# Fused attention, gated MLP and mixer on one core: the opening rebuilt (whole-float32 first product, masks by TensorE, keys copied by GpSimd, a new order)

## The chip, the cores and the metric

The kernel runs on one core of one Trainium2 chip. The metric is the device time of one execution in microseconds. Everything is one launch: attention, then a gated MLP with a spatial mix, then a token mixer and a channel mixer.

## The reference, cut to what matters

```python
# q, k, v: (4, 8, 576, 64); a causal window of 64 keys
scores = 0.125 * q @ k^T;  scores = where(0 <= t - s < 64, scores, -1e9)
x = softmax(scores) @ v                        # heads joined: (4, 576, 512)
h = relu(x @ w_in);  u, v = h[..., :512], h[..., 512:]       # w_in (512, 1024)
v_n = (v - mean(v)) / sqrt(var(v) + 1e-6)      # over the 512 features
v_s = einsum('ts,bsd->btd', w_spatial, v_n) + b_spatial
x = (u * v_s) @ w_out
h = relu(x^T @ w_tok1) @ w_tok2;  u = x + h^T                # mixes the 576 tokens
out = u + relu(u @ w_ch1) @ w_ch2              # mixes the 512 channels
```

The weights of the two MLPs arrive as 64-bit floats; the kernel takes them apart into 32-bit words itself.

## The kernel before, in words

**Arithmetic.** A product is held accurate by splitting each operand into a rounded part in the reduced float32 format that TensorE takes in one pass (`hi`) and the rest (`lo`), and adding three products, hi·hi, hi·lo and lo·hi (`mm3`, L200). Scores, transposes and probability-times-value use plain float32 operands.

**Attention turns.** The queries are cut into 18 turns of 128 rows. For each pair of batches p there are nine: `i = 0` takes the two 64-row tails of the two batches, `i = 1..8` the eight whole tiles. Before the change they run in the order 0 to 17. A turn n has these steps, whose names appear in the prediction: `Lq` loads queries and keys (L265 for a tile, 640 KB; L267 for tails, 768 KB); `Lv` loads values (L272, 512 KB); `S` is the 32 score matmuls (L295), which run on quarters of the array; `M` on DVE adds the mask and takes the row maximum (L309, per half of the heads, so eight instructions a turn); `X` on ACT is the exponential with its row sum (L318); `I` on DVE is the reciprocal of the sums (L326, L327); `N` multiplies it in, on POOL for turns 0 to 9 (`EARLY`) and on DVE later (L330); `T` transposes (L520) and `C` copies out of PSUM (L525 on DVE or L527 on ACT, by `CD0` and `CD1`); `V` is the 32 matmuls with the values (L338); `xh` and `xl` split the result (L585 ACT, L590 DVE). Then `v`, the 12 matmuls 128x512 with the right half of `w_in` (L200), and for each three turns four `u` products of 12 matmuls 128x384 with its left half. `v` goes on to `R` (relu, ACT), `bn` (DVE), `rs` (POOL), `ts` (DVE, L392), `hi` (ACT) and `lo` (DVE, L398). Spatial products `s` follow when a batch has all its tiles.

**`w_in`.** It comes in eight pieces of 512 KB: `w_v` 0 to 3 (rows of the right half) and `w_u` 0 to 3. A piece is loaded into a spare stretch of the big tile `U` (`wL`, L444), scaled by ACT (`wd`, L153), joined from its two words by two DVE instructions (`wo`, L453 and L454), rounded by ACT (`wh`, L457) and its rest taken by DVE (`wl`, L459). Seven pieces are formed in a PSUM bank of the ring `mm`, which has three; piece `u1` (`PU`) is formed in place in SBUF, with its rest taken by POOL (L472 to L477).

**Who decides the order.** `plan()` states every step of this stage with an engine, a rank, a planned duration, what it comes after and what buffers it takes (`sp` 4 PSUM banks, `xo` 1, `mm` 3, `qk` 2 and `v` 2 buffers, and so on), and `Steps.run()` lists the steps in time by those planned numbers. Each engine then executes its steps in exactly that order, waiting in line for each. The queue SP has a fixed list for the first loads (`ORDER` indexes `loads`), into which a load outside the list can go when the head of the list has no buffer yet. `PADS` and `WARM` put stand-in matmuls (`keep_busy`, L247, 128x512 in bfloat16, results unused) into TensorE's order ahead of named steps. After the plan come the rest of the spatial products, the output product, the token mixer and the channel mixer, none of which the change touches.

Of the kernel before, what the change touches and what calls it, by code (L numbers as in the profile page):

```python
# [36 lines left out]
RANK = dict(M=0.96, X=5.22, I=-0.72, N=6.15, T=0.48, C=1.04, xh=3.48, xl=-0.6, R=0.29, bn=3.08, ts=0.44, hi=4.2, lo=5.8, E=1.49, G=-4.23, av=3.48, dv=1.82, au=4.89, du=3.49, aw=2.75, dw=1.67, c2=4.58)  # L37
SLACK = dict(cd=0.38, cs=0.3, ch=2.95, cl=0.35, oh=0.73, ol=0.69, aw=2.46, ws=2.23, sums=0.17, wd=0, X=0, N=0.3, T=0.32, C=0.14, xh=0.03, xl=0.01, R=0.6, bn=1.03, ts=0.21, hi=0.54, lo=1.64, E=0.9, G=0.2)
# [10 lines left out]
class Steps:  # L49
# [14 lines left out]
    def start(self, step):  # L64
        name, eng, rank, us, fn, after, take, give, hold, kb = step
        at = self.clock.get(eng, 0.0)
        lag = self.LAG + SLACK.get(name[0], 0.0)
        for a in after:
            if a not in self.done:
                return None  # L70
            at = max(at, self.done[a] + lag)
        for r in set(take):
            free, n = sorted(self.room[r]), take.count(r)
            if len(free) < n:
                return None
            at = max(at, free[n - 1] + self.LAG)
        return max(at, self.lands[-8 + (kb > 520)]) if kb else at

    def run(self):
        while True:  # L80
# [32 lines left out]
def tile_kernel(ctx, tc, qk, qkE, v, w_u, w_v, wsT, b_sp, w_out, w_t1, w_t2, w_c1, w_c2, outT):  # L113
# [22 lines left out]
    const.tile([P, 24], F32, name="gap")  # L136
# [112 lines left out]
    its = [(p, i) for p in range(B // 2) for i in range(9)]  # L249
    held, vheld, soft, xt, vn = {}, {}, {}, {}, {}  # L250
# [5 lines left out]
    def qk_parts(t, n):  # L256

        width = 192 if its[n][1] else 256
        return t[:, :512].rearrange("p (j t) -> p j t", j=4), t[:, 512:512 + 4 * width].rearrange("p (j k) -> p j k", k=width)

    def load_qk(n):
        p, i = its[n]
        t = att.tile([P, 1536], F32, tag="qk", name="qk")
        if i:
            nc.sync.dma_start(out=t[:, :1280], in_=qk[8 * p + i - 1])  # L265
        else:
            nc.sync.dma_start(out=t, in_=qkE[p])  # L267
        held[n] = qk_parts(t, n)

    def load_v(n):  # L270
        t = att.tile([P, 1024], F32, tag="vv", name="vv")
        nc.sync.dma_start(out=t, in_=v[n])  # L272
        vheld[n] = (t[:, :512], t[:, 512:])

    def scores(n, pad=0):

        p, i = its[n]
        if n >= len(its):  # L280
            return
        qq, kk = held.pop(n)
        step = 64 if i else 128
        which = 1 if i and where(p, i)[1] == 0 else 0
        on_pe = n < MASK_PE
        scs = [psa.tile([P, 4, 128], F32, tag="sp", name="sc") for _ in range(2)]
        keep_busy(pad, scs[0])
        if on_pe:
            for sc in scs:
                nc.tensor.matmul(sc, ident16, msk16[:, which].unsqueeze(1).to_broadcast([P, 4, 128]), start=True, stop=False)  # L290
        for j in range(4):
            for q in range(2):
                for e in range(2):
                    er = slice(64 * e, 64 * e + 64)
                    nc.tensor.matmul(scs[e][64 * q:64 * q + 64, j, :], qq[er, j, 64 * q:64 * q + 64],  # L295
                                     kk[er, j, step * q:step * q + 128], start=not on_pe, stop=not on_pe or j == 3)
        pb = att.tile([P, 8, 128], F32, tag="pb", name="pb", bufs=PB)
        nm = att.tile([P, 8], F32, tag="nm", name="nm", bufs=3)
        sm = att.tile([P, 8], F32, tag="sm", name="sm", bufs=3)
        soft[n] = (scs, pb, nm, sm, None if on_pe else msk16[:, which])  # L300
# [20 lines left out]
    def snorm(n, g=None):  # L321
        pb, sm = soft[n][1], soft[n][3]
        hs = slice(0, 8) if g is None else slice(4 * g, 4 * g + 4)
        w = hs.stop - hs.start
        rs = att.tile([P, 8], F32, tag="rs", name="rs", bufs=4)[:, :w]
        nc.vector.tensor_scalar(out=rs, in0=sm[:, hs], scalar1=1e-9, scalar2=None, op0=ALU.add)  # L326
# [3 lines left out]
        eng.tensor_tensor(out=pb[:, hs, :], in0=pb[:, hs, :], in1=rs.unsqueeze(2).to_broadcast([P, w, 128]), op=ALU.mult)  # L330
# [43 lines left out]
    def uv_v_mm(p, i, ps):  # L374
# [3 lines left out]
        mm3(ps, [(xh[:, k, ts_], xl[:, k, ts_], wi_h[:, k, 512:], wi_l[:, k, 512:]) for k in range(4)], late=(0, 1, 2) if p + i > 1 else (0, 2, 1))  # L378

    def norm_parts(p, i, ps, vv):  # L380
# [9 lines left out]
        nc.gpsimd.tensor_tensor(out=rstd, in0=rstd, in1=mhalf, op=ALU.pow)  # L390
        yield
        nc.vector.tensor_scalar(out=vv, in0=vv, scalar1=mv[:, 0:1], scalar2=rstd, op0=ALU.subtract, op1=ALU.mult)  # L392
        yield
        if i:
            h, l = turn(nh_ring), turn(nl_ring)
            nc.scalar.copy(out=h, in_=vv)
# [5 lines left out]
        for at in (0, 64):  # L402
            h, t = turn(nh_ring), turn(tail_ring)
            nc.scalar.copy(out=h[at:at + 64], in_=vv[at:at + 64])
            nc.scalar.copy(out=t[:64], in_=vv[at:at + 64])
            hs.append((h, t))
        yield
        for at, (h, t) in zip((0, 64), hs):
# [32 lines left out]
    def w_part(raw, src, hi, lo, cols):  # L441

        raw = raw.bitcast(I32)
        nc.sync.dma_start(out=raw, in_=src.bitcast(I32))  # L444
        r3 = raw.rearrange("p (a c w) -> p a c w", a=4, w=2)
        low, high = r3[:, :, :, 0], r3[:, :, :, 1]
        yield
        ps = psmm.tile([P, 512], F32, tag="mm", name="mm")
        y = ps.rearrange("p (a c) -> p a c", a=4)
        down(y, high)  # L450
        yield
        y = y.bitcast(I32)
        nc.vector.tensor_scalar(out=y, in0=y, scalar1=3, scalar2=None, op0=ALU.logical_shift_left)  # L453
        nc.vector.scalar_tensor_tensor(out=y, in0=low, scalar=29, in1=y, op0=ALU.logical_shift_right, op1=ALU.bitwise_or)  # L454
        yield
        v3 = ps.rearrange("p (k c) -> p k c", c=cols)
        nc.scalar.copy(out=hi, in_=v3)  # L457
        yield
        nc.vector.tensor_tensor(out=lo, in0=v3, in1=f(hi), op=ALU.subtract)  # L459

    def wu_pool(ft):

        fs = slice(128 * ft, 128 * ft + 128)
        raw = U[:, ft, :1024]
# [10 lines left out]
        nc.scalar.copy(out=hi, in_=x)  # L475
        yield
        nc.gpsimd.tensor_tensor(out=lo, in0=x, in1=f(hi), op=ALU.subtract)  # L477

    def wu_part(ft):
        fs = slice(128 * ft, 128 * ft + 128)  # L480
        return w_part(U[:, ft, :1024], w_u[ft], wi_h[:, :, fs], wi_l[:, :, fs], 128)

    def wv_part(k):
# [890 lines left out]
```

## Time and profile before

| | |
|---|---|
| median of three runs | 612.3 us (612.06 to 615.5) |
| the profiled execution | 610.2 us, of which span 608.4 us |
| PE busy | 599.8 us (99%), 4419 matmuls |
| DVE, ACT, POOL busy | 468.9, 350.0, 135.5 us (77%, 58%, 22%) |
| DMA | 108.06 MB, mean 178 GB/s |
| granted TensorE clock | 1.00 throughout |
| chain that ended last | PE 93%, DMA 4%, DVE 1%, ACT 1% |

The span runs from the first to the last instruction. "Busy" of PE includes the stand-in matmuls, and the end of a matmul in the records includes its way through the array, so a row of matmuls back to back is read by its length in the chain of waits rather than by the sum of its members.

### The profile page before, as it was taken

How to read it: one execution, taken by the hardware profiler on the slowest of the kernel's cores; microseconds unless marked ns; L12 is line 12 of the kernel's file. 1: busy time of each engine (PE TensorE's matmuls, PEld its weight loads, DVE VectorE, ACT ScalarE, POOL GpSimd, SP SyncE). 2: the span in 40 equal slices, each digit the busy share in tenths (PEclk: the TensorE clock that was granted, in tenths of full speed). 3: DMA queues.
4: the chain of work that ended last, by engine and by line, in shares of the span. 5: the costliest groups of instructions: out<-in, count | busy, mean ns of one | idle time of the engine just before them, and what ended most of it. 6: DMA issues, size and time to landing. Idle time of an engine off the chain costs nothing.

```text
span 608.4 us, 12236 instructions
## 1 busy us (share of the span) xinstructions
PE 599.8 (99%) x4419; PEld 560.3 (92%) x4419; DVE 468.9 (77%) x1124; ACT 350.0 (58%) x883; POOL 135.5 (22%) x166
## 2 busy tenths in 40 slices
PE   8899999999999999999999999999999999999997
PEld 4688998998898998788988999999999999999997
DVE  5998798989788655594478877878877889786982
ACT  6997678768696334663254445556463647454540
POOL 5342341322233000231046011140012140021310
PEclk9999999999999999999999999999999999999999
DMA  8955269777545803416021314665515675434772
GB/s 351 375 173 181 95 225 312 246 253 267 200 146 210 264 38 94 133 71 207 20 86 63 120 61 145 243 218 209 177 64 192 210 267 169 152 102 176 251 260 79
DMA packets 43093, 108.06 MB, mean 178 GB/s; under 512 B 4372, under 2 KB 14872, under 8 KB 43032
## 3 DMA queue, kind: packets, MB, share of 16 engines
q1 hardware_dynamic: 43032, 107.27, 51.3%
q8 instruction: 35, 0.57, 0.4%
q14 instruction: 26, 0.21, 0.1%
HBM read 86.81 MB, written 20.45 MB: 176 GB/s over the span
## 4 chain that ended last, share of the span: by engine, by line
PE 93%; DMA 4%; DVE 1%; ACT 1%; issue 0%; ACTq 0%
PE mm L200 36%; PE A L1220 19%; PE mm L1008 12%; PE A L1008 9%; PE A L200 6%; PE sc L295 3%; PE sp L520 2%; DMA qk<-in_qk 2%; PE xo L338 2%; PE A L926 1%; PE mm L338 1%; DMA k<-sums 1%; PE A L1304 1%; DMA qk<-in_qkE 1%; DVE pb L309 0%; ACT sh L187 0%
## 5 line engine op out<-in xcount | busy, mean ns | idle before, releaser
L1220 PE MATMUL A<-room,w 128*128 128x384 f32 x720 | 130.0, 334 | 0.0
L1220 PEld LDWEIGHTS A<-room,w 128*128 128x128 f32 x720 | 125.3, 188 | 0.0
L1002 POOL TENSOR_TENSOR hid<-hid 128x384 f32<-128x384 f32 x36 | 42.3, 1186 | 204.0 <-DVE hid L1002 155.6
L1214 ACT CAST room<-hid 128x384 fp32r<-128x384 f32 x120 | 60.9, 513 | 45.4 <-PE A L1220 40.3
L1215 DVE TENSOR_TENSOR room<-hid,room 128x384 fp32r<-128x384 f32 x120 | 71.5, 622 | 12.5 <-ACT room L1214 9.6
L200 PE MATMUL mm<-ws,room 128*128 128x288 f32 x416 | 60.6, 297 | 0.0
L318 ACT ACTIVATE pb<-pb,nm 128x128 f32<-128x128 f32 x144 | 55.8, 393 | 6.9 <-DVE nm L309 6.7
L1033 ACT ACTIVATE hid<-hid 128x384 f32<-128x384 f32 x54 | 28.2, 525 | 53.1 <-DVE hid L1036 53.1
L200 PEld LDWEIGHTS mm<-ws,room 128*128 128x128 f32 x416 | 56.8, 188 | 0.5 <-issue 0.2
L1036 DVE TENSOR_TENSOR hid<-A,hid 128x384 f32<-128x384 f32 x54 | 29.4, 552 | 19.8 <-PE A L1008 14.6
L1008 PE MATMUL mm<-room,sh 128*128 128x384 f32 x144 | 36.5, 334 | 0.0
L309 DVE CUSTOM_DVE_ANT_0 pb<-sc,msk 128x128 f32<-128x128 f32 x144 | 31.5, 284 | 5.8 <-PE sc L295 5.8
L200 PE MATMUL mm<-xh,wi_h 128*128 128x384 f32 x96 | 33.2, 346 | 0.0
L866 POOL TENSOR_TENSOR k<-k 128x256 f32<-128x256 f32 x12 | 9.8, 833 | 105.0 <-ACT gh L907 57.2
L200 PE MATMUL mm<-xh,wi_l 128*128 128x384 f32 x96 | 32.2, 336 | 0.0
L200 PE MATMUL mm<-xl,wi_h 128*128 128x384 f32 x96 | 32.1, 335 | 0.0
L330 POOL TENSOR_TENSOR pb<-pb,rs 128x512 f32<-128x512 f32 x20 | 21.6, 1083 | 41.6 <-DVE rs L327 20.7
L200 PE MATMUL mm<-gh,wo_h 128*128 128x512 f32 (+1 forms) x80 | 30.2, 378 | 0.0
L200 PE MATMUL mm<-gl,wo_h 128*128 128x512 f32 (+1 forms) x80 | 29.6, 370 | 0.2 <-DVE gl L908 0.2
L908 DVE TENSOR_TENSOR gl<-U,gh 128x512 fp32r<-128x512 f32 (+1 forms) x20 | 13.3, 666 | 21.1 <-ACT gh L907 21.0
L200 PE MATMUL mm<-gh,wo_l 128*128 128x512 f32 (+1 forms) x80 | 29.5, 369 | 0.0
L1245 DVE TENSOR_TENSOR U<-A,U 128x384 f32<-128x384 f32 x42 | 21.9, 550 | 9.3 <-PE A L1220 4.7
(183 smaller groups left out, 1507.3 us busy)
## 6 DMA issues: line engine op xcount, KB each, us to landing
w<-scr SPq DMA_DIRECT2D x63, 512.0 KB, 4.1
scr<-raw SPq DMA_DIRECT2D x48, 256.0 KB, 3.2
qk<-in_qk SPq DMA_DIRECT2D x16, 640.0 KB, 6.6
vv<-in_v SPq DMA_DIRECT2D x18, 512.0 KB, 5.4
k<-sums SPq DMA_DIRECT2D x18, 512.0 KB, 3.5
craw<-in_w_c SPq DMA_DIRECT2D x24, 256.0 KB, 3.1
outT<-U SPq DMA_DIRECT2D x24, 192.0 KB, 1.9
k<-in_w_c SPq DMA_DIRECT2D x6, 512.0 KB, 3.5
```

Source lines behind the costliest of these rows:

```text
L200: nc.tensor.matmul(o, a, c, start=(i == 0), stop=(i == n - 1))
L309: nc.vector.tensor_tensor_reduce(out=pb[:, 4 * g + h, :], in0=scs[g][:, h, :], in1=mk, scale=-SCALE, scalar=3e38, op0=ALU.add, op1=ALU.min ...
L318: nc.scalar.activation(out=pb[:, h, :], in_=scs[g][:, h - 4 * g, :] if mk is None else pb[:, h, :], func=AF.Exp, scale=SCALE if mk is None ...
L330: eng.tensor_tensor(out=pb[:, hs, :], in0=pb[:, hs, :], in1=rs.unsqueeze(2).to_broadcast([P, w, 128]), op=ALU.mult)
L1002: eng.tensor_tensor(out=out, in0=a, in1=b, op=ALU.subtract)
L1008: nc.tensor.matmul(o, a, m, start=first and i == 0, stop=i == len(todo) - 1, skip_group_check=True)
L1033: nc.scalar.activation(out=o, in_=src, func=AF.Relu)
L1036: nc.vector.tensor_tensor(out=o, in0=a, in1=b, op=ALU.add)
L1214: nc.scalar.copy(out=oh, in_=blk[j])
L1215: nc.vector.tensor_tensor(out=ol, in0=blk[j], in1=f(oh), op=ALU.subtract)
L1220: nc.tensor.matmul(acc[d], a, m, start=(first and j == 0 and i == 0), stop=(last and j == NJ - 1 and i == 2), skip_group_check=True)
L1245: nc.vector.tensor_tensor(out=at, in0=src, in1=at, op=ALU.add)
```

## The change

- **First product whole.** `NV = 1`: the `v` product of turn 0 is four plain float32 matmuls, 128x512, from a float32 copy of `x` (new ACT step `xf`) and the joined words of `w_v`, in place of twelve of the split kind. It waits for the four `wo` steps, not for `wh` and `wl`; turn 0 still has its `xh` and `xl`, for the `u` products.
- **Masks by TensorE.** `MASK_PE = 3`: for turns 0 to 2 two bfloat16 matmuls 128x512 put the mask into the score banks ahead of the scores; DVE takes the maximum by one `tensor_reduce` per half and scales it, and ACT's exponential reads PSUM and writes SBUF. The banks come free after `X`, not after `M`. Code for this stood in the kernel before, unused.
- **Keys and values.** A tile is laid out as [64 old keys, 128 new keys, queries]. For turns 0 to 5 (`KN = 6`) that are tiles, the old keys are not loaded where they are zeros (POOL `memset`) or lie in the buffer of the turn before (POOL copy, step `Ko`): turns 0, 1, 4 and 5, 128 KB less each. For turns 0 and 1 the 64 rows that both halves of the values share are loaded once and copied by POOL (`Vo`): 384 KB in two DMAs.
- **Order of turns.** `FIRST = (1, 2, 0)`: two whole tiles first, the tails third. Turn 0's queries come in two DMAs of 64 partitions each, and its scores in two steps, one for each (`S 0,0` and `S 0,1`).
- **`w_in` in SBUF.** All eight pieces are formed in place in `U` (`w_piece`), none in PSUM; the rests of `v2` and `u3` are taken by POOL.
- **Later work.** For turns 5 to 13 (`HP`) the `hi` copy of a tile goes from ACT to POOL; for turn 17 (`TA`) ACT normalises in place of DVE; from turn 11 on (`IM`) `I` is one step for both halves; `C` of turns 2 and 3 (first half) and 3 to 5 (second half) is on DVE. The switches `IP`, `TP`, `WP` are empty, so their code does not run.
- **Order.** `ORDER`, `RANK`, `SLACK`, `PADS` and `WARM` are new, and with them the order of every engine in this stage. The loads in SP's list now go: `w_v0`, queries 0 in two halves, values 0, queries 1, `w_v2`, queries 2, `w_v3`, queries 3, `w_v1`, `w_u0`, values 1, `w_u2`, `w_u3`, `w_u1`. Before: queries 0 and 1, `w_v2`, values 0, `w_v1`, `w_v0`, queries 2, `w_v3`, queries 3, `w_u0`, values 1, `w_u2`, `w_u3`, `w_u1`.

The diff, cut to its core:

```diff
-MASK_PE = 0
+MASK_PE = 3
-WARM = 9
-PADS = {("S", 1): 5, ("T", 0, 0): 12, ("T", 0, 1): 3, ("T", 1, 1): 2, ("S", 4): 4}
+WARM = 7
+PADS = {("T", 0, 0): 4, ("S", 2): 7, ("S", 4): 4}
-CD0 = range(0, 1)
-CD1 = range(3, 8)
-PU = (1,)
-ORDER = (0, 2, 5, 4, 3, 1, 7, 6, 10, 9, 8, 12, 13, 11)
+CD0 = range(2, 4)
+CD1 = range(3, 6)
+PV = (2,)
+NV = 1
+FIRST = (1, 2, 0)
+KN = 6
+VN = 3
+HP = range(5, 14)
+IM = 11
+TA = range(17, 22)
+PU = (3,)
+ORDER = (2, 0, 1, 5, 3, 6, 8, 7, 11, 4, 10, 9, 13, 14, 12)
...
+    its = [(0, i) for i in FIRST] + [(p, i) for p in range(B // 2) for i in range(9) if p or i > 2]
...
+    def form_keys(n):
+        old = tile_of(n)[:, :256]
+        if old_keys(n) == "zero":
+            nc.gpsimd.memset(old, 0.0)
+        else:
+            last = qk_tiles[n - 1][:, 256:768].rearrange("p (j k) -> p j k", j=4)[:, :, 64:]
+            nc.gpsimd.tensor_copy(out=old.rearrange("p (j k) -> p j k", j=4), in_=last)
...
+    def form_v(n):
+        va, vb = vheld[n]
+        nc.gpsimd.tensor_copy(out=vb[:64], in_=va[64:])
...
         if on_pe:
-            for sc in scs:
-                nc.tensor.matmul(sc, ident16, msk16[:, which].unsqueeze(1).to_broadcast([P, 4, 128]), start=True, stop=False)
+            for e in es:
+                nc.tensor.matmul(scs[e], ident16, msk16[:, which].unsqueeze(1).to_broadcast([P, 4, 128]), start=True, stop=False)
...
+    def uv_v_whole(x, ps):
+
+        for k in range(4):
+            w = U[:, k, 1152:2176].rearrange("p (c w) -> p c w", w=2)[:, :, 1]
+            nc.tensor.matmul(ps, x[:, 128 * k:128 * k + 128], w, start=k == 0, stop=k == 3)
...
+    def w_piece(raw, src, hi, lo, eng, cast):
+
+        words = raw.rearrange("p (a c w) -> p a c w", a=4, w=2)
+        x, y, low = words[:, :, :, 1], words.bitcast(I32)[:, :, :, 1], words.bitcast(I32)[:, :, :, 0]
+        nc.sync.dma_start(out=raw.bitcast(I32), in_=src.bitcast(I32))
+        yield
+        down(x, y)
+        yield
         nc.vector.tensor_scalar(out=y, in0=y, scalar1=3, scalar2=None, op0=ALU.logical_shift_left)
         nc.vector.scalar_tensor_tensor(out=y, in0=low, scalar=29, in1=y, op0=ALU.logical_shift_right, op1=ALU.bitwise_or)
         yield
-        v3 = ps.rearrange("p (k c) -> p k c", c=cols)
-        nc.scalar.copy(out=hi, in_=v3)
-        yield
-        nc.vector.tensor_tensor(out=lo, in0=v3, in1=f(hi), op=ALU.subtract)
+        (nc.gpsimd.tensor_copy if cast else nc.scalar.copy)(out=hi, in_=x)
+        yield
+        eng.tensor_tensor(out=lo, in0=x, in1=f(hi), op=ALU.subtract)
...
-            nc.scalar.copy(out=h, in_=vv)
+            (nc.gpsimd.tensor_copy if at_turn[p, i] in HP else nc.scalar.copy)(out=h, in_=vv)
...
+            if n < NV:
+                S.add(("v", n), "PE", 10, 3.65, product, after=[("xf", n)] + [("wo", "v", k) for k in range(4)], take=["mm"], give=["vf"], hold=3.5, line="work")
+            else:
+                S.add(("v", n), "PE", 10, 2.95, product, after=[("xl", n)] + [("wl", "v", k) for k in range(4)], take=["mm"], hold=2.83, line="work")
```

## Rows read from the trace of the kernel before

**Rows 1.** Windows: stretch, busy time of each engine (instructions), granted clock, DMA share, GB/s.
```profile
0.00:10.00 10.00, 8.82 (x86) 4.12 (x87) 3.36 (x30) 4.57 (x17) 4.73 (x19) 1.00 0.81 315
10.00:20.00 10.00, 8.41 (x125) 5.39 (x123) 9.66 (x39) 9.98 (x38) 4.12 (x4) 1.00 1.03 387
20.00:30.00 10.00, 8.26 (x120) 6.17 (x118) 9.79 (x49) 10.00 (x41) 4.17 (x4) 1.00 0.97 384
30.00:60.00 30.00, 30.00 (x326) 26.34 (x321) 26.55 (x96) 25.22 (x81) 10.34 (x14) 1.00 0.54 173
```

**Rows 2.** Waits of PE after 29 us: total us, times, longest.
```profile
PE xo L338 <- DVE xl L590: 1.1, 1, 1.1
```

**Rows 3.** Timeline of PE: start, us, engine, line, what, [idle before].
```profile
5.10 1.10 PE L295 MATMUL sc<-qk 64*64 64x128 f32 x32
6.14 1.25 PE L247 MATMUL sc<-warm 128*128 128x512 bf16 x5
...
14.51 1.23 PE L295 MATMUL sc<-qk 64*64 64x128 f32 x32 [0.35 <-DMA qk<-in_qk]
...
16.26 1.15 PE L338 MATMUL xo<-PT,vv 128*64 128x64 f32 x32
...
21.43 1.49 PE L295 MATMUL sc<-qk 64*64 64x128 f32 x32 [0.66 <-DMA qk<-in_qk]
...
24.97 1.17 PE L200 MATMUL mm<-wi_h,xh 128*128 128x512 f32 x4
...
29.03 1.15 PE L338 MATMUL xo<-PT,vv 128*64 128x64 f32 x32 [1.08 <-DVE xl L590]
```

**Rows 4.** Windows, stand-in matmuls (L247) alone.
```profile
0.00:29.03 29.03, 10.40 (x35) 3.40 (x35) 1.00 0.94 361
```

**Rows 5.** Chain of waits, PE: start, us, what.
```profile
49.23 2.76 PE mm L200 x12
51.98 1.08 PE xo L338 x32
...
54.00 1.91 PE sc L295 x64
...
66.66 0.44 PE sp L520 x4
```

**Rows 6.** Chain of waits: the query loads.
```profile
6.29 8.08 DMA qk<-in_qk
...
15.80 5.59 DMA qk<-in_qk
```

**Rows 7.** Timeline of DVE: fourth piece of `w_v`, joined and split.
```profile
20.38 0.69 DVE L454 SCALAR_TENSOR_TENSOR mm<-U,mm 128x512 int32<-128x512 int32 x1
...
23.80 0.68 DVE L459 TENSOR_TENSOR wi_l<-mm,wi_h 128x512 fp32r<-128x512 f32 x1
```

**Rows 8.** By line: what `w_in` costs; count, then ns min/median/max.
```profile
L453 DVE TENSOR_SCALAR mm<-mm x7: 673/689/693, 10.6 to 34.2; 128x512 int32<-128x512 int32 x7
...
L472 DVE TENSOR_SCALAR U<-U x1: 422/422/422, 35.5 to 35.5; 128x512 int32<-128x512 int32 x1
...
L457 ACT CAST wi_h<-mm x7: 581/587/624, 12.0 to 35.9; 128x512 fp32r<-128x512 f32 x7
...
L475 ACT CAST wi_h<-U x1: 677/677/677, 37.5 to 37.5; 128x512 fp32r<-128x512 f32 x1
...
L477 POOL TENSOR_TENSOR wi_l<-U,wi_h x1: 1304/1304/1304, 38.2 to 38.2; 128x512 fp32r<-128x512 f32 x1
```

**Rows 9.** By line: DVE operations between SBUF tiles.
```profile
L392 DVE TENSOR_SCALAR vf<-vf,mv,rstd x18: 516/544/1417, 36.9 to 198.1; 128x512 f32<-128x512 f32 x18
...
L398 DVE TENSOR_TENSOR room<-vf,room x16: 659/684/1221, 48.9 to 201.5; 128x512 fp32r<-128x512 f32 x16
```

**Rows 10.** Timeline of POOL: last constant, first normalisations.
```profile
4.61 1.17 POOL L226 CAST tails<-U 64x512 fp32r<-64x512 f32 x2
...
12.41 2.04 POOL L330 TENSOR_TENSOR pb<-pb,rs 128x512 f32<-128x512 f32 x2 [0.53 <-DVE rs L326]
```

More of the change, by code (lines that the diff above doesn't have):

```diff
@@ L252, in where, with tile_of @@
     def where(p, i):
         return (2 * p + (i - 1) // 4, (i - 1) % 4) if i else (None, None)
[L256 to L261, printed above, removed]
-        p, i = its[n]
-        t = att.tile([P, 1536], F32, tag="qk", name="qk")
+    def tile_of(n):
+        if n not in qk_tiles:
+            qk_tiles[n] = att.tile([P, 1536], F32, tag="qk", name="qk")
+        return qk_tiles[n]
@@ new lines, in old_keys @@
+    def old_keys(n):
+        p, i = its[n]
+        if not i or n >= KN:
+            return None
+        return "zero" if where(p, i)[1] == 0 else "copy" if n and its[n - 1] == (p, i - 1) else None
+    def form_keys(n):
[5 more added lines that the diff above has]
+            nc.gpsimd.tensor_copy(out=old.rearrange("p (j k) -> p j k", j=4), in_=last)
@@ L297, in scores @@
[L297 to L300, printed above, removed]
+                    nc.tensor.matmul(scs[e][64 * q:64 * q + 64, j, :].rearrange("p (w k) -> p w k", w=2), qq[er, 128 * j + 64 * q:128 * j + 64 * q + 64],
+                                     keys_of(n, er, j, q), start=not on_pe, stop=not on_pe or j == 3)
@@ new lines, in load_values, with has_keys, scored @@
+        def load_values(n):
+            part = its[n][1] and n < VN
+            S.add(("Lv", n), "SP", 8 + 2 * n, 0, lambda: load_v(n), take=["v"], hold=0.95 if part else 0.5, kb=385 if part else 512, line="SP" if n < 2 else None)
+            if part:
+                S.add(("Vo", n), "POOL", -1, 0.8, lambda: form_v(n), after=[("Lv", n)], hold=0.75)
+        def has_keys(n):
+            return [("Lq", n)] + [("Ko", n)] * (old_keys(n) is not None)
+        def scored(n, es=(0, 1)):
+            scores(n, S.pad, es)
@@ L558, in block @@
             ahead = [m for m in (n + len(ns), n + len(ns) + 1)[:len(ns)] if m <= last] if len(ns) > 1 else [n + 2]
-            need = [("C", m, g) for m in ns for g in range(2)] + [("Lv", m) for m in ns]
+            need = [("C", m, g) for m in ns for g in range(2)] + [("Vo" if its[m][1] and m < VN else "Lv", m) for m in ns]
             if len(ns) > 1:
-                need += [("Lq", m) for m in ahead]
+                need += [x for m in ahead for x in has_keys(m)]
             else:
@@ L569, in product @@
                 att_pv(m, held.pop(("PT", m)), xo.rearrange("p (j t) -> p j t", j=4))
[L571 removed]
+            take = ["xo"] + ["mm"] * (len(ns) - 1) + ["XT"] * sum(m % 3 == 0 for m in ns) + ["sp", "sp", "pb"] * len(ahead)
             for m in ns:
```

231 lines of the change are left out of this document (140 added, 91 removed).

## The prediction

> **What bounds the kernel now.** I read the busy time by stretch first, then the waits of TensorE (PE), then its timeline over the opening, then the loads.
>
> From 30 to 60 us PE has 30.00 of 30 us busy, while ACT has 25.22 and DVE 26.55 [rows 1]. Past 29 us the longest wait of PE is 1.1 us, and that is the one which ends at 29.03 [rows 2, 3]. From there to the tail the time is PE's work laid end to end, so a step that becomes faster on another engine there buys nothing, and the later part of the change (`HP`, `TA`, `IM`, the copies of `C`) I cost at nothing; its cover is ACT's and DVE's slack of 3 to 5 us in each 30.
>
> Before 29.03 it is otherwise. PE seems busy, but 10.40 us of that are stand-ins [rows 4]. Its real work there is the scores `S` of turns 0 to 4, six half-turn `T`, `V` of two turns and one `v`. At the lengths these have back to back (`S` 1.91/2 = 0.955, `T` 0.44, `V` 1.08, `v` 2.76 [rows 5]) this is 4.78 + 2.64 + 2.16 + 2.76 = 12.3 us. So **16.7 us of the opening are lost**, and the change can win only there. What fills the opening: from 10 to 30 ACT is busy 9.98 and 10.00 of 10, DVE 9.66 and 9.79, the DMA engines all the time at 387 and 384 GB/s [rows 1]. Three resources are full together. The first `v` starts at 24.97 [rows 3], right behind the last rest of `w_v`, which begins at 23.80 and takes 0.68; the words of that piece were joined by 20.38 + 0.69 = 21.07 [rows 7]. The scores of turns 2 and 4 wait for query loads that take 8.08 and 5.59 us from issue [rows 3, 6].
>
> **The change, part by part.**
>
> *Loads.* At 315, 387 and 384 GB/s, 3.15 MB have moved by 10 us, 7.02 by 20 [rows 1]. In the order of issue the queries of turn 2 end at 4.19 MB, which these rates reach at 12.7; they landed at 6.29 + 8.08 = 14.4. Those of turn 4 end at 7.08 MB, reached at 20.2, landed at 21.4 [rows 6]. So a landing is this sum and about 1.5 us. In the new order, with whole tiles first (512 KB, then 384 KB of values, then 512), turn 2 ends at 3.80 MB, turn 3 at 4.98, the fourth `w_v` piece at 5.51, turn 4 at 6.55, values 1 at 6.95. This counts the values of turn 2 ahead of the queries of turn 2, as a load outside the list can slip in while the head has no buffer; without it all are 0.52 MB, 1.4 us, sooner. Landings with it: 13.1, 16.2, 17.5, 20.2 and 21.3. The fourth piece of `w_v`, put behind three turns of queries, lands between 16.1 and 17.5; I take 16.8.
>
> *First product whole.* It needs no `wh` and `wl`, which were 24.97 - 21.07 = 3.9 us of the path. New path: 16.8, then `wd` about 0.6 (the ACT pass over the same 128x512 in SBUF, L475, takes 0.68 [rows 8]), then 0.42 for the shift in SBUF [rows 8] and 0.69 to join [rows 7], and 0.5 for an ACT and DVE that are never idle: **it starts at 19.0**. Its other operand, `xf`, costs ACT one more pass of about 0.59 (L457 [rows 8]) and is ready long before: turn 0's `V` was at 16.26 [rows 3] and comes no later. No row shows a plain float32 matmul of 128x512. Below, the `V` rows: 32 plain float32 matmuls of 64 columns, two at a time on half the array each, in 1.08 us is 1.05 ns a column, and 4 x 512 columns are 2.16 us. Above, four half-products at the rate at which `mm3` does three: 2.76 x 4/3 = 3.68. I take 3.68, as it comes from the row with the same tile: 0.92 more than now; the other end would be 0.60 less.
>
> *Masks by TensorE.* Six bfloat16 matmuls of 128x512 at 0.25 each (five in 1.25 [rows 3]) are 1.5 us on PE. They stand ahead of scores that wait for their queries, where stand-ins stood before; cost nothing. If the cover goes, 1.5. On DVE one reduction over 128x512 (no row; between 0.52, a pass of SBUF [rows 9], and 0.69, one of PSUM [rows 8]) and a small scaling replace four instructions; nothing either way. ACT reads PSUM in place of SBUF; rows for 128x512 casts are 0.587 from PSUM against 0.677 from SBUF [rows 8], so at most a seventh of six half-turn exponentials, 1 us; at least nothing. I take nothing.
>
> *`w_in` in SBUF.* The shift falls from 0.689 to 0.422 [rows 8], 0.27 on DVE for each of about five pieces before 29 us, 1.3. One `wl` moves to POOL, 0.68 off DVE, at 1.30 on POOL [rows 8]. `w_v0` is now the first load and can be taken apart before the first scores, while ACT and DVE have nothing (by 10 us they had worked 4.57 and 3.36 [rows 1]): 2.1 us off DVE's full stretch, 1.2 off ACT's. In sum DVE gets back 4.1 us. ACT gets back 1.2 and pays 0.59 for `xf` and 0.09 more for each cast out of SBUF, some 0.5: nothing in sum. That is why I do not let the stretch end sooner than the loads allow. The freed PSUM banks remove no wait that the rows show.
>
> *Keys and values by POOL, tails third.* The first scores need the keys' `memset`, which stands in POOL's order behind constants that end at 4.61 + 1.17 = 5.78 [rows 10]; the `memset` is at most 0.5. The scores begin at 6.3 in place of 5.10 [rows 3], and end near 8, as one half of the heads fills half of the array at a time. Behind them wait `M`, `X`, and the load of turn 2. SP issues three more DMAs, in time in which it waits for buffers anyway. The late start of `X` costs nothing as long as `V` of turn 0 is not what `v` waits for; ACT uses the time for `w_v0`. `Vo` and `Ko` add some 0.5 to 0.8 us each to POOL, which had worked 4.1 of 10 us [rows 1].
>
> *The sum.* Before 19.0 PE does four `S` (turn 3's queries are there at 16.2), four `T`, one `V`: 3.82 + 1.76 + 1.08 = 6.66. From 19.0 to 29.03 it has `v`, then `T` and `V` of turns 1 and 2, `S` of turn 4, two more `v`, enough to be full but for one wait, for values 1 (21.3) and their split; I put 1 us for it. Useful, measured in the old work: 10.03 - 0.92 - 1 = 8.1. Together 14.8 against 12.3: **2.4 us gained**. Past 29 us nothing changes. The profiled execution took 610.2 us (span 608.4), 2.1 under the median of the three runs; 607.8 for such an execution, **609.9 as a median**.
>
> **Rivals.**
>
> *Everything on time.* The fourth piece lands at 16.1, nothing waits, no gap after: `v` at 17.8, useful 6.66 + 11.2 - 0.92 = 17.0, a gain of 4.6 us, 607.7; with the cheap float32 rate 6.1, 606.2. For it: the path has slack on DVE now. Against it: ACT, full and not relieved.
>
> *The saving in loads is paid back.* Turn 0's queries come as two transfers of 64 partitions, and the values of turns 0 and 1 likewise in parts. No row shows the rate of a large transfer to half the partitions. If each half runs at half the rate, 0.52 + 0.39 MB ahead of everything else cost 1.3 + 1.0 = 2.3 us more, and every later landing slips by it: the gain of 2.4 is gone, 612.2. The Trainium skill's page SBUF — State Buffer ("Can I just issue two DMAs to hit both halves?") says just this: a transfer to partitions 0 to 63 reaches half of the ports, and two such transfers serialize. Against it: the queue holds other whole-width loads at the same time, and its engines were at full rate with loads of several kinds in flight [rows 1].
>
> *Slower: DVE waits for POOL.* A DVE pass between SBUF tiles takes 0.544 as a rule and 1.417 at worst, a subtraction 0.684 and 1.221 [rows 9]; POOL held a 1.04 us instruction in such cases. Seven pieces leave PSUM for SBUF: some 19 DVE instructions that were out of POOL's reach (0.673 to 0.693 without exception [rows 8]) come into it, and POOL's share of the time rises from 4.1 of 10 us to about 6. At 0.6 of the time and some 0.7 us for each meeting (between 0.54 and 0.87), 19 x 0.6 x 0.7 = 8 us are lost, 4.1 got back: the joined words are 3.9 us late, `v` starts at 25.0 as before and pays 0.92, and the second `v`, which still needs all four `wl`, adds a gap of 1: 1.9 slower, 614.2. It decides from about 6.5 us lost, where the gain is gone. The Trainium skill's GPSIMD Engine Reference (Key points) states the contention for two-port modes and for two SBUF inputs, both of which hold here; the rows above agree for the worst cases, but the medians beside them say that most instructions meet nothing, and many POOL instructions lie where DVE reads PSUM.
>
> **How the numbers follow.** A measurement of this kernel can tell about 1% (6 us) from no change. Chances: forecast (gain 0.8 to 3.5) 0.48; everything on time (3.5 to 7) 0.25; loads paid back (within 0.8) 0.13; slower 0.14. The range runs from the far end of the second, with the cheap float32 rate and 1 us for the unknown exponential, 605.2, to the third and most of the last, 614.2. Faster by over 1% (below 606.2) needs that far end, half of the second case: 0.13. Slower by over 1% needs losses past every row here: 0.04.
>
> **What would show it.** In the changed kernel: first plain float32 `v` at 18 to 20 us and 3.7 long, from four matmuls; PE without waits of over 1 us afterwards; stand-ins down to 22, hence less than 7 us; the shifts of `w_in` at 0.42, not 1.0 or more; first scores at 6.3. Wrong if `v` starts past 22, if the second `v` is more than 3 us behind the first's end, or if PE shows waits after 30 us that it had not.

## The result, and the profile after

The changed kernel takes 617.1 us (median of 10 executions, 614.4 to 619.1), the kernel before 612.35 beside it (10 executions): ratio 1.0078 [1.0054, 1.0101]. It is 4.8 us slower; the forecast was 609.9, its range 605.2 to 614.2. The profiled execution of the changed kernel took 619.0 us (span 617.2), 1.9 above its median, as the one of before was 2.1 below its own. The two traces are thus 8.8 us apart, 4 us more than the medians; sizes below that matter are taken from medians, and the traces show places. In the experiments a few executions of 846 us and more, one of them the profiled one of e3, are left out of the medians and ratios.

The busy time by stretch, as in [rows 1] (length of the stretch; PE, PEld, DVE, ACT, POOL; then granted clock, DMA share, GB/s):

```profile
0.00:10.00 10.00, 8.05 (x41) 4.29 (x41) 3.46 (x6) 3.86 (x10) 6.68 (x23) 1.00 0.82 247
10.00:20.00 10.00, 10.00 (x101) 6.02 (x100) 7.03 (x19) 7.72 (x32) 4.50 (x5) 1.00 1.00 360
20.00:30.00 10.00, 7.23 (x122) 5.02 (x122) 7.92 (x31) 9.23 (x34) 3.28 (x5) 0.83 0.84 297
30.00:60.00 30.00, 28.26 (x308) 23.10 (x307) 27.45 (x81) 24.07 (x78) 11.35 (x14) 1.00 0.51 161
```

The three resources that were full together from 10 to 30 us are not so any more: ACT has 7.72 and 9.23, DVE 7.03 and 7.92, and the DMA engines are full from 10 to 20 us and at 0.84 behind. Up to 30 us ACT did 20.81 us of work and DVE 18.41, against 24.55 and 22.81 before. Some of DVE's difference is work that the change saves (shorter shifts, one rest moved to POOL); what is not saved has to be done later. PE, in time, answering to [rows 3]:

```profile
1.04 3.17 PE L261 MATMUL mm<-warm 128*128 128x512 bf16 x7 [1.04 <-DVE warm L138]
4.98 0.58 PE L342 MATMUL sc<-msk,ident 128*128 128x512 bf16 x1 [0.77 <-POOL msk L145]
5.71 1.97 PE L347 MATMUL sc<-qk 64*64 64x128 f32 x16
7.61 0.61 PE L342 MATMUL sc<-msk,ident 128*128 128x512 bf16 x1
8.15 1.97 PE L347 MATMUL sc<-qk 64*64 64x128 f32 x16
10.05 1.03 PE L342 MATMUL sc<-msk,ident 128*128 128x512 bf16 x2
11.02 1.99 PE L347 MATMUL sc<-qk 64*64 64x128 f32 x32
...
17.46 1.10 PE L347 MATMUL sc<-qk 64*64 64x128 f32 x32
...
25.36 1.69 PE L261 MATMUL sc<-warm 128*128 128x512 bf16 x4 [2.77 <-DVE nm L357]
26.98 1.99 PE L347 MATMUL sc<-qk 64*64 64x128 f32 x32
28.89 0.69 PE L572 MATMUL sp<-ident,pb 128*128 128x128 f32 x4
29.52 1.15 PE L394 MATMUL xo<-PT,vv 128*64 128x64 f32 x32
30.60 3.87 PE L440 MATMUL mm<-U,xf 128*128 128x512 f32 x8
```

The first scores are two steps of 1.97, where 32 took 1.10; turn 1's begin at 11.02 in place of 7.32, turn 2's at 17.46 in place of 14.51. At 25.36 a stop of 2.77 ends: stand-ins and scores of turn 4 wait for the banks that the maxima of turn 3 (L357, DVE) give free, and behind them in PE's line stand a `T` of turn 2, `V` of turn 1 and the first `v`, at 30.60 (24.97 before, 19.0 forecast). What DVE and ACT waited for longest from 3 to 30 us (total us, times, longest):

```profile
DVE mx L354 <- PE sc L347: 4.1, 4, 1.7
DVE U L531 <- ACT U L167: 3.9, 1, 3.9
DVE pb L357 <- PE sc L347: 1.3, 1, 1.3
```

```profile
ACT wi_h L534 <- DVE U L532: 2.3, 2, 1.5
ACT U L167 <- DMA U<-in_w_v: 2.2, 1, 2.2
ACT pb L366 <- DVE rs L378: 1.8, 2, 0.9
ACT pb L366 <- DVE nm L361: 1.7, 1, 1.7
```

In the kernel before the two waited in that stretch for the first scores (ACT 4.7, DVE 5.8), and then hardly at all. The gap is whole by 60 us: the first pair of scores (turns 6 and 7) begins at 59.59 in place of 53.93 with one `v` less behind it, 5.66 + 2.76 = 8.4 us of the 8.8. From this pair to the end are 557.6 us here and 556.6 to 559.2 in the traces of e1, e2, e5 to e8, e14, e18 and e19, which put the same work ahead of it: what they gain is gained before it.

### The profile page after: what moved, and what is told of

Read it like the earlier page. It is cut to its first block, busy times and chain, and to the rows that moved or that the text cites. A ratio compares the mean times of both kernels' runs of the same rounds, so it can differ in the third digit from the quotient of the medians.

```text
span 617.2 us, 12189 instructions
## 1 busy us (share of the span) xinstructions
PE 606.2 (98%) x4408; PEld 563.8 (91%) x4408; DVE 469.6 (76%) x1071; ACT 348.3 (56%) x878; POOL 144.7 (23%) x184
## 4 chain that ended last, share of the span: by engine, by line
PE 91%; DVE 4%; DMA 2%; ACT 1%; issue 1%; POOL 0%; SPq 0%; ACTq 0%; POOLq 0%; DVEq 0%
PE mm L214 34%; PE A L1315 19%; PE mm L1103 12%; PE A L1103 9%; PE A L214 6%; PE sc L347 3%; PE sp L572 2%; PE A L1021 1%; DMA k<-sums 1%; PE mm L394 1%; PE xo L394 1%; PE A L1399 1%; DVE U L532 1%; DMA qk<-in_qk 1%; DVE pb L357 1%
## 5 line engine op out<-in xcount | busy, mean ns | idle before, releaser
L366 ACT ACTIVATE pb<-pb,nm 128x128 f32<-128x128 f32 x120 | 46.7, 395 | 4.0 <-DVE nm L357 4.0
L202 DVE TENSOR_TENSOR sl<-k,sh 128x1024 fp32r<-128x1024 f32 x18 | 25.8, 1436 | 2.7 <-PE mm L1103 1.2
```

Source lines behind the costliest of these rows:

```text
L202: eng.tensor_tensor(out=lo, in0=x, in1=f(hi), op=ALU.subtract)
L366: nc.scalar.activation(out=pb[:, h, :], in_=scs[g][:, h - 4 * g, :] if mk is None else pb[:, h, :], func=AF.Exp, scale=SCALE if mk is None ...
```

## The experiments

All times are medians, given in the order of the list above them; each ratio is to the kernel before on the same chip, with its 95% interval.

**Single edits of the changed kernel.** Theory C: the two warm-up products that it dropped let the opening run at the lower rate. Theory P: the stand-ins ahead of turn 4's scores delay the work behind them.

```
e1_warm9           WARM = 7 -> 9
e2_nopad4          PADS without ("S", 4): 4
e3_warm9_nopad4    both
e4_before_warm7    the kernel before: WARM = 9 -> 7
```

> The changed kernel with 9 opening stand-ins in place of 7, nothing else; the planned order is the same. Theory C (cold TensorE): the changed kernel leaves a 0.77 us gap between its last stand-in and the first mask, and runs at the 1.2 GHz length (a 128x512 stand-in 0.47 us, 32 scores 1.99 us) from 5 to about 15 us; with 9 the scores of turn 0 come at full rate, 16 of them in about 1.0 us in place of 1.97, they end near 7.8 in place of 10.1, the load of turn 2 goes out 2.4 us sooner, and the time falls by 2 to 4 us to 613 to 615. Theory D (DVE waits for POOL in SBUF) and theory L (order of loads): the clock is a by-product; below 1 us, 616 to 617.

> The changed kernel without the four stand-ins ahead of the scores of turn 4. They write the score bank, so they wait for the same bank as the scores (PE idle 2.77 us until 25.36) and then run 1.69 us in front of them. Theory P (the stand-ins lie on the path): the scores of turn 4 start at 25.4 in place of 27.0, the first product near 28.9 in place of 30.6, time 1.5 to 2 us less, 615 to 615.6. Rival: the first product waits for the fourth joined piece of w_v (27.8) and the engines behind it, so that below 1 us is gained, 616 to 617; or the clock stays down longer without them, and it is slower.

> Both edits: 9 opening stand-ins, none ahead of the scores of turn 4. If theories C and P both hold and are separate, the two gains add: 3.5 to 6 us, 611 to 613.5. If C removes the wait that P removes, the sum is less than that by over 1 us. If D or L is the cause, 615.5 to 617.

> The kernel before with 7 opening stand-ins in place of 9, nothing else. Theory C: 7 end at about 4.1, the first scores wait for their load until 5.1, TensorE stays at the 1.2 GHz length until the stand-ins ahead of the scores of turn 1 and the first transposes bring it up; the scores of turn 0 take about 2 us, the first product starts 1 to 2 us late, 613 to 614.5. Rival: the gap does not matter there, 612 to 612.6.

Measured: 616.16 (1.0068 [1.0051, 1.0085]); 616.97 (1.0088 [1.007, 1.0106]); 615.2 (1.0054 [1.0036, 1.0071]); 613.22 (1.0019 [1.0005, 1.0033]). With nine warm-up products PE shows:

```profile
5.66 1.09 PE L347 MATMUL sc<-qk 64*64 64x128 f32 x16
6.69 0.39 PE L342 MATMUL sc<-msk,ident 128*128 128x512 bf16 x1
7.01 1.09 PE L347 MATMUL sc<-qk 64*64 64x128 f32 x16
...
26.17 3.87 PE L440 MATMUL mm<-U,xf 128*128 128x512 f32 x8
```

The three scores take 3.28 us in place of 5.93, and `v` comes 4.4 us sooner. This trace is of the fastest of six executions (615.0) and that of the changed kernel of its second slowest (619.0), so the 4.4 stand beside 4.0 us of these two and not beside the medians. By the medians the time gains 1.0 (0.6 by the ratios, with intervals that overlap); the kernel before loses 1.2 [0.3, 2.0] by the opposite edit, so there C is surely something, about 1 us. P is worth nothing that can be told: e2 lies 0.1 under the changed kernel, e3 1.0 under e1, within the intervals.

**Four parts undone, added up.** Theory H: transfers to half of the partitions slow the loads. Rival: POOL's rests hold up DVE.

```
e5_whole_loads    e1; turn 0's queries and the values of turns 0, 1 in whole transfers, no copy by POOL
e6_dve_low        e1; rests of w_v 2, w_u 3 on DVE
e7_whole_scores   e5; scores of turn 0 as one step of 32
e8_four           e1 + e5 + e6 + e7, and no stand-ins ahead of S4
```

> The changed kernel with 9 opening stand-ins, and the queries of turn 0 and the values of turns 0 and 1 loaded over all 128 partitions in one transfer each (128 KB more for each value, no value copy on POOL); the planned order is the same. Theory H (transfers to 64 partitions are slow): from 5 to 10 us the DMA engines are full in both, at 307 GB/s with halves and 407 in the kernel before; here the rate goes back to about 400, the fourth w_v piece lands 1.5 to 2 us sooner, the first product starts near 24.5 in place of 26.2, the time falls by 1 to 2 us from 616.2, to 614 to 615.2. Rival: the rate comes from the rows or from waits for buffers and stays near 310, time 616 to 617.

> The changed kernel with 9 opening stand-ins, and the rests of w_v2 and w_u3 taken by DVE (0.69 us each) in place of POOL (1.3 to 1.75); the planned order of all else is the same. Theory D (DVE waits for POOL in SBUF): POOL's 1.75 us instruction at 18.8 made three DVE instructions wait (0.43, 0.77 and 0.67 us in place of 0.42, 0.69 and 0.16), so the gain is 0.5 to 1 us, 615.2 to 615.7; if contention were the main loss, 2 us or more. Rival: DVE's own 0.69 more in a full stretch cancels it, 616 to 616.6.

> As the run with whole-width loads, and the scores of turn 0 in one step of 32 in place of two of 16. Half the heads use half the rows of the array: 16 take 1.09 us where 32 take 1.10. Expected: the scores of turn 0 end 1 us sooner, the query load of turn 2 goes out 1 us sooner, 0.3 to 1 us off that run. Rival: the fourth w_v piece and the order behind it decide, no change beyond 0.3 us.

> All together: 9 opening stand-ins, whole-width loads, scores of turn 0 in one step, rests by DVE, no stand-ins ahead of the scores of turn 4. If clock, half-width transfers and contention are what the change lost by, the first product starts below 23 us and the time is at the kernel before or under it, 609 to 612.5. If the new order itself (the waits in line behind the scores of turn 4 and the fourth w_v piece) is the cause, it stays above, 613.5 to 615.

Measured: 615.9 (1.0061 [1.004, 1.0081]); 616.0 (1.0067 [1.0044, 1.0089]); 615.89 (1.0059 [1.0037, 1.0081]); 613.92 (1.0036 [1.0021, 1.005]). The stretch from 5 to 10 us, of the changed kernel and then of e5:

```profile
5.00:10.00 5.00, 4.86 (x34) 3.25 (x33) 3.15 (x5) 1.93 (x8) 2.77 (x4) 1.00 1.03 304
```

```profile
5.00:10.00 5.00, 5.00 (x70) 3.34 (x69) 3.71 (x9) 2.48 (x12) 2.14 (x3) 1.00 1.04 415
```

The last column confirms H as a rate, 304 GB/s against 415 (407 in the kernel before) with the DMA engines busy all the time in both. The time does not follow: 0.3 us, within the intervals. None of the three alone moves it; together, with the stand-ins ahead of S4 gone as well, they give back 2.2 (616.2 to 613.9, with intervals that do not overlap). In e8 PE still stops ahead of S4, the scores of turn 4:

```profile
22.59 1.99 PE L352 MATMUL sc<-qk 64*64 64x128 f32 x32 [3.10 <-DVE nm L362]
24.50 1.12 PE L577 MATMUL sp<-ident,pb 128*128 128x128 f32 x4
25.55 1.98 PE L399 MATMUL xo<-PT,vv 128*64 128x64 f32 x32
27.46 4.33 PE L445 MATMUL mm<-U,xf 128*128 128x512 f32 x8
```

A stop of 3.10 is followed by scores of 1.99 (1.10 at the full rate), a `T` of 1.12 (0.66), a `V` of 1.98 (1.15) and a `v` of 4.33 (3.87): 2.6 us more. The granted clock from 22.59 to 27.46 is 0.50, the lower of its two levels (1.2 GHz of 2.4).

**New plans.** Theory L: what is left is PE's line, S4 ahead of `V` and `v`, and DVE's, the maxima of turn 3 ahead of the fourth `w_v` join.

```
e9_join_first          e8:        M(3): after=[... , ("wo", "v", 1)]
e13_after_join_first   changed:   the same line
e10_split              e8:        NV = 1 -> 0
e11_old_order          e8:        RANK, SLACK, CD0, CD1 and ORDER as in the kernel before
```

> The kernel of four undone parts (nine warm-up products, whole loads, unsplit scores, both rests back on DVE, no stand-ins ahead of turn 4's scores), and one line more: the maxima of turn 3 may not be planned ahead of the join of the last w_v piece. On DVE that join then stands ahead of M(3), and on TensorE the scores of turn 4 fall behind V of turn 1 and the first v. Theory L (line): TensorE stood 3.10 us because S4 was in its line ahead of work that was ready, and DVE joined the fourth piece at 24.83 because M(3) was in its line ahead of it; so the first v begins at 22.8 to 24.5 in place of 27.46, TensorE has no wait over 1.5 us from 19 to 30, and the time is 610 to 612 (613.92 without the line). Rival N (new parts cost as such): the wait goes to another instruction and the time stays at 613.5 to 614.5. Rival F (the clock): v begins sooner but runs at 4.3 us or longer, and the time gains under 1 us.

> The changed kernel with that one line alone: the maxima of turn 3 not ahead of the join of the last w_v piece. Theory L: the first v, at 30.60 in the changed kernel, begins at 26 to 28, and the time falls from 617.1 to 613 to 615. Rival N: the fourth piece is late for other reasons (cold opening, half-width loads), v begins past 29 and the time stays at 616 to 617.5.

> The kernel of four undone parts with the whole float32 product undone as well: the first v is made of three products like the others. Theory L: TensorE's line holds the first v behind S4 whichever way it is formed, so the whole product gained nothing of its start; with rests to wait for, v begins at 27 to 29 and the time is 613 to 615. Rival W: the whole product, 0.92 us dearer, is itself the loss: 612 to 613. Rival E (the product does what it is for): v begins 3 us or more later than 27.46 and the time is 615.5 to 617.

> The kernel of four undone parts with the ranks, the allowances, the places of the copies of C and the order of loads of the kernel before. All of the new mechanisms stay: whole product, masks by TensorE, tails third, w_in in SBUF. Theory L: in this line the first v stands ahead of V of turn 1 and the fourth w_v piece is loaded ahead of the queries of turns 2 and 3; v begins at 21 to 24.5 and the time is 610.5 to 613. Rival N: 614 to 616, since the new parts cost as much under any order.

Measured: 618.26 (three executions, 616.9 to 621.1; 1.0111 [1.0074, 1.0147]); 617.16 (1.0087 [1.0065, 1.011]); 617.2 (1.0084 [1.0058, 1.0111]); 620.9 (1.0149 [1.0114, 1.0183]). `v` began at 25.17, 27.11, 34.06 and 23.65. It was earlier in three of them, in e11 and e13 by as much as theory L said and in e9 by 0.7 less, and by its median none is faster: e11 has the earliest `v` of these and the longest time. The theory falls as it was put. These runs settle less than they should, as one line makes a new plan: in e9 PE stops again for 2.25 at 39 us, and it is idle for 2.08 of the 50 us from 150.

**One part alone, the order kept.** Parts of the change put into the kernel before, whose planned order stays as it was; and e8 with eighteen steps moved by hand in the finished plan.

```
e15_before_sbuf    w_part forms the piece in U and not in a PSUM bank
e16_before_masks   MASK_PE = 3 in scores, smax, sexp; 0 in the plan
e17_before_whole   e15; v of turn 0 by four float32 products from U and xf
e14_hand_order     e8; xf, xh, xl of turn 0, C of turn 1, wo of the fourth piece earlier;
                   S4 behind the first v, maxima of turn 4 behind xl of turn 1
```

> The kernel before with one part of the change: all pieces of w_in formed in SBUF and not in PSUM; the planned order is kept to the last instruction. Theory D (DVE meets POOL in SBUF): some shifts, joins and rests are drawn out by 0.3 to 0.9 us, DVE loses 1.5 to 3 us in the opening, the first v begins at 25.5 to 27 (24.97 before), and the time is 613 to 615.5. Rival M (the rows of before: the medians of SBUF passes are shorter): v begins at 24 to 25.2 and the time is 611 to 612.8.

> The kernel before with one part of the change: the masks of three turns by TensorE; the planned order is kept to the last instruction. My prediction costed this at nothing: 611.8 to 612.9. Rival B (banks): with exponentials read from PSUM the banks of the scores come free after X and not after M, some 1.6 us later, so a transposition or the scores of turn 4 begin later: 613.5 to 615.5. Rival G (a gain on DVE, one reduction and a scaling in place of eight passes): 610 to 611.5.

> The kernel before with w_in formed in SBUF and the first product with w_v in whole float32 (one more copy on ACT); the planned order is kept, so the first v stays behind V of turn 1 in TensorE's line. If the whole product does what I predicted, v begins at 22 to 24 and 3.7 long, and the time is 0.5 to 2 us under that of the same kernel without it. If TensorE's line or a join is its gate, v begins past 24.5 and the time is 0.5 to 1.5 us above that kernel's.

> The kernel of four undone parts, with its planned order kept to the last instruction but for eighteen steps around 17 to 27 us that are moved by hand: both copies and the rest of turn 0's output and the C of turn 1 come earlier on ACT and DVE, the words of the fourth w_v piece ahead of those of w_u and of the maxima of turn 3, and on TensorE V of turn 1 and the first v ahead of the scores of turn 4. Theory L (the lines alone): V of turn 1 begins at 20.3 to 21.5 (25.55 without the moves), the first v at 22 to 24 (27.46), no stop over 1.3 us and no stretch at the lower clock between 17 and 30; 609.5 to 611.5 against 613.9 without the moves. Theory D (DVE is too slow, whatever stands first in its line): v at 24 or later, TensorE stops again for 2 us or more before 40 us, 613 to 615.

Measured: 612.82 (1.0 [0.9987, 1.0012]); 615.95 (1.006 [1.0039, 1.008]); 613.39 (1.0012 [0.9996, 1.0028]); 616.12 (1.0055 [1.0036, 1.0074]). The pieces in SBUF cost nothing that can be told (0.0 [-0.8, +0.7]), and neither does the whole product; but it gains nothing here either: `v` begins at 26.77 in the trace of e17 and at 26.66 in that of e15, in both right behind `V` of turn 1 and a `T` in PE's line. The masks cost 3.7 [2.4, 4.9]. ACT in e16, its first two lines:

```profile
8.31 1.28 ACT L319 ACT_TABLE_LOAD   x1 [8.31 <-DVE nm L314]
9.60 0.37 ACT L319 ACTIVATE pb<-sc,nm 128x128 f32<-128x128 f32 x1
```

and PE, two of the waits that are new and the first `v`, 2.98 later than before:

```profile
11.16 2.75 PE L248 MATMUL sp<-warm 128*128 128x512 bf16 x12 [1.24 <-ACT pb L319]
...
23.89 1.02 PE L248 MATMUL sc<-warm 128*128 128x512 bf16 x4 [0.79 <-ACT pb L319]
...
27.95 1.18 PE L201 MATMUL mm<-wi_h,xh 128*128 128x512 f32 x4
```

The first exponential begins 2.89 us later than before (6.71). Of that 1.28 is the table load, which in e16 stands behind the maximum and elsewhere runs at 0.72: a by-product of this edit alone, as in the changed kernel ACT has a piece of `w_v` ahead. Some 1.1 is the two products ahead of the scores, with the scores themselves at 1.43 in place of 1.10, and 0.5 that one reduction ends later than the first of four passes. The two waits for ACT are the rival "banks" of the expectation: exponentials that read PSUM hold the banks until `X`. If the table load costs its whole length, which no run shows, about 2.4 of the 3.7 belongs to the masks. e14 is slower than any of its forecasts; PE:

```profile
23.87 1.73 PE L415 MATMUL xo<-PT,vv 128*64 128x64 f32 x32 [3.36 <-DMA vv<-in_v]
```

With S4 out of the way `V` of turn 1 stops as long, for its values: their load stood behind that of turn 2's values, which had slipped into the list, and so behind `V` of turn 0. Part of the 616.1 goes with the clock: with the same program, the four executions of e14 at a mean granted clock of 1.000 took 614.3 to 615.9, the four at 0.993 or 0.994 616.5 to 618.6.

**The last two.** The masks undone in the changed kernel with its order kept; and e14 with masks undone and the values of turn 1 loaded ahead of turn 2's, those of turn 0 behind two other loads.

```
e18_after_no_masks   MASK_PE = 0 in scores, smax, sexp; 3 in the plan
e19_loads_order      e14 with that, and Lv(1) ahead of Lv(2), Lv(0) behind the second w_v piece
```

> The changed kernel with one part undone: the masks of the first three turns are added by DVE again; the planned order is kept to the last instruction. Theory B (banks): the masks by TensorE cost the kernel before 3.7 us, as exponentials that read PSUM hold the banks of the scores until X, and as their products stand ahead of the first scores. If that is also the changed kernel's loss, the stop ahead of turn 4's scores (2.77 us) and the waits for the masks go, and the time is 612.5 to 615 (617.1 with the masks). Rival O (the order and the loads set the opening whatever frees the banks): 616 to 617.5.

> The kernel with eighteen steps moved by hand, and two changes more: masks on DVE again as in the run beside it, and three loads moved (the values of turn 1 ahead of those of turn 2, which had slipped in front of four other loads and left the values of turn 1 to wait for V of turn 0; the values of turn 0 behind the queries of turn 1 and a w_v piece). Theory B and the loads together: V of turn 1 no longer waits 3.36 us for its values and begins at 20 to 21.5 (23.87 without), the first v at 21.5 to 23.5 and 3.7 long, no stretch at the lower clock from 17 to 30; 608.5 to 611.5, at or below the kernel before. If the wait only moves to a join on DVE, v begins past 24.5 and the time is 612 to 614.5.

Measured: 616.01 (1.0066 [1.0044, 1.0088]), 1.1 under the changed kernel (0.7 by the ratios) with intervals that overlap, and 613.79 (1.0024 [1.001, 1.0038]). PE in e19:

```profile
20.40 1.15 PE L416 MATMUL xo<-PT,vv 128*64 128x64 f32 x32 [1.26 <-DMA vv<-in_v]
21.48 0.66 PE L594 MATMUL sp<-ident,pb 128*128 128x128 f32 x4
21.97 3.76 PE L462 MATMUL mm<-U,xf 128*128 128x512 f32 x8
...
29.99 0.56 PE L369 MATMUL sc<-qk 64*64 64x128 f32 x2 [2.20 <-DVE nm L379]
30.88 1.98 PE L369 MATMUL sc<-qk 64*64 64x128 f32 x30 [0.33 <-DVE nm L379]
32.79 1.98 PE L416 MATMUL xo<-PT,vv 128*64 128x64 f32 x32
34.69 2.08 PE L231 MATMUL mm<-wi_h,xh 128*128 128x512 f32 x4
```

Everything up to 25.66 is where the expectation had it, `v` 3.0 us ahead of the kernel before, ACT with 24.59 us of work by 30 us (24.55 before). Then the scores of turn 5 stop for 2.20 + 0.33 us behind the maxima of turn 4, which I had moved back to make room, and three groups run at the lower rate (granted clock 0.51 from 29.99 to 34.69): 0.88 + 0.83 + 0.90 = 2.6 us more. No version beat the kernel before. Whether this one would with those maxima put forward again was not tried.

## Why the prediction was wrong

The step that failed first is the path to the first `v`, with its term "0.5 for an ACT and DVE that are never idle", and the sum built on it: the gain was reckoned from the start of the first `v`, and its start from the landing of the fourth piece of `w_v` at 16.8 and three passes. In the trace those passes queue. DVE's lines, where the second pair is the fourth piece, and ACT's pass over that piece:

```profile
20.34 1.00 DVE L361 TENSOR_SCALAR nm<-mx 128x4 f32<-128x4 f32 x1
21.26 0.42 DVE L531 TENSOR_SCALAR U<-U 128x512 int32<-128x512 int32 x1
21.71 0.69 DVE L532 SCALAR_TENSOR_TENSOR U<-U 128x512 int32<-128x512 int32 x1
...
26.67 0.41 DVE L531 TENSOR_SCALAR U<-U 128x512 int32<-128x512 int32 x1
27.12 0.69 DVE L532 SCALAR_TENSOR_TENSOR U<-U 128x512 int32<-128x512 int32 x1
```

```profile
24.98 0.68 ACT L167 ACTIVATE U<-U 128x512 f32<-128x512 f32 x1
```

ACT scales it at 24.98, behind a piece of `w_u`, `xf`, `xh` and a `C`; DVE joins it by 27.8 (forecast 19.0), behind `M` of turn 3 and `xl`; and `v` follows at 30.6, behind S4, `T` and `V` in PE's line. The landing was put too early as well: the changed kernel has moved 2.47 MB by 10 us and 6.07 by 20, where the prediction took 3.15 and 7.02 from the kernel before. Its own sum (5.51 MB, and 1.5 us) then gives 19.9, an estimate, as the trace has no landing for this piece. So of the 11.6 us some 3 are the loads and the rest the lines of ACT, DVE and PE. And the start of `v` does not set the time anyway: in the profiled executions of the changed kernel, e1, e8, e19 and e11, `v` at 30.60, 26.17, 27.46, 21.97 and 23.65 went with 619.0, 615.0, 614.0, 614.1 and 619.7, and 24.97 with 610.2 before.

*"The late start of X costs nothing as long as V of turn 0 is not what v waits for; ACT uses the time for w_v0."* This failed too, as far as the runs can tell. The prediction itself had ACT full from 10 to 30 us; what such an engine misses ahead of the stretch has to be made up behind it. The exponentials begin at 8.72 (6.71 before), those of turn 2 at 20.15 (17.63), and `V` of turn 0, which was to come no later than 16.26, at 19.52. Up to 30 us the changed kernel's ACT is 3.7 us behind, near the 4.8 that are lost. Over all the profiled executions but that of e3 this is a tendency and no law: with 20.4 to 22.0 us of ACT work by 30 us (the changed kernel, e2, e5, e7, e11, e13, e16, e18) they took 616.2 to 619.7, with 22.1 to 22.7 (e1, e4, e6, e8) 613.8 to 615.0, with 23.2 to 24.6 (the kernel before, e15, e17, e19) 610.2 to 614.1; but e9, e10 and e14 had 22.7 to 23.5 and took 618.3 to 621.1.

*Masks "cost nothing".* The place of the stand-ins gave the cover for PE's 1.5 us, and no step asked when the banks come free. In the kernel before they cost 3.7, perhaps 2.4 without the table load; in the changed kernel, taking them out gives 1.1, not surely different from nothing.

*Two warm-up products fewer* were not costed at all: about 1 us, sure in the kernel before only.

*The split scores* had the right mechanism: half of the heads take as long as all (1.09 against 1.10 in e1), and at the full rate they end at 8.1, as forecast. In the changed kernel they end at 10.1.

*Right.* The whole product: 3.70 us (from 30.60 to 34.30) for a forecast of 3.68. Its gain: none in the kernel before; e10 puts it at 3 us in the new order, mixed up with a new plan. The shift in SBUF takes 0.40 to 0.43. "Past 29 us nothing changes" holds from 60 us on only: from 30 to 60 PE is busy for 28.26 of 30 us, with a wait of 1.43 at 49.9.

*The rivals.* "Loads paid back" named the right mechanism: half-width transfers run at 304 GB/s where whole ones run at 415. The rule of the Trainium skill, SBUF — State Buffer ("Can I just issue two DMAs to hit both halves?"), agrees with this trace in direction; the rate is 0.73 of the other, not half of it, with other loads in flight. As a price it was wrong: whole transfers gave 0.3 us. "DVE waits for POOL" is seen as well, in passes of 1.00 and 0.92 that take 0.17 and 0.16 elsewhere, and rests of 1.12 and 1.34 against 0.68; but e15 brings DVE within reach of POOL in the old order, and costs 0.0 [-0.8, +0.7] us. The Trainium skill's GPSIMD Engine Reference (Key points) is right about the meeting; it tells nothing of whether anybody waits for the pass that was drawn out.

**What stays open.** Of 4.8 us, about 1 is the warm-up by the medians, about 2 come back when three further parts and the stand-ins are undone with it (616.2 to 613.9), and about 2 remain in e8 (1.0036). For that rest the traces show stops of 2.2 to 3.4 us, each with a stretch at the lower rate after it; each time one was removed another came, so it is argued and not shown that the order alone is to blame. Not all of the loss is the lower rate behind stops: the two executions of the changed kernel at a mean granted clock of 1.000 took 614.4 and 616.4, the five at 0.989 to 0.997 617.0 to 619.1, and the kernel before takes 612.35. The order of the turns and the keys by POOL (`FIRST`, `KN`) were never undone alone.

## What to carry to other kernels

Where several engines are full together, do not price a change by the start of one late instruction: count the work that each full engine has done by the end of the stretch, and ask of each edit whether it leaves one of them idle, at the beginning above all. An edit that makes another unit read a buffer also moves the time at which the buffer comes free; follow that to whoever waits for it. To tell a part from the order around it, put the part alone into the old kernel with the old order held fixed: that gave sharp answers here, where every new plan moved hundreds of steps and blurred its own question. And hold what a trace shows against the time of that execution: the executions of one kernel lay up to 5 us apart here, as much as the change was worth.

## What the runs showed of the hardware that was not expected

- Scores on 64 of the rows, for half of the heads, take as long as for all: 16 in 1.09 us, 32 in 1.10. The two halves of the array had been working side by side.
- From 3 to 11 us the changed kernel's row says a granted clock of 1.00, while 16 scores take 1.97 in place of 1.09. The trace has no record of the clock there: its first one, at the full level, begins at 15.4 us (at 5.6 in e1, at 4.7 in the kernel before and at 9.7 in e4), and a stretch without a record counts as 1.00 in this column. After the stop at 22.6 to 25.4 the row does show the lower level:

```profile
3.00:11.00 8.00, 7.09 (x39) 3.68 (x37) 4.09 (x8) 2.81 (x10) 4.48 (x11) 1.00 1.02 314
...
22.60:25.40 2.80, 0.04 (x1) 0.05 (x2) 2.41 (x11) 2.80 (x6) 1.04 (x1) 1.00 0.93 259
25.40:30.60 5.20, 5.20 (x73) 3.40 (x73) 3.59 (x22) 5.20 (x21) 0.61 (x1) 0.67 0.98 347
```

  So in an opening the level is read from the lengths of known instructions. Ahead of 25.4 to 30.6 PE had stood for 2.8 us.
- A table load of 1.28 us on ACT can take over the wait of the instruction behind it: at 0.72 in the kernel before, at 8.31 in e16.
